# Attention and mixture of experts in one kernel: transposes, value products, sums and gates of a unit moved into two slots

## The chip, the cores and the metric

The kernel runs on one core of one Trainium2 chip. The metric is the device time of one execution in microseconds. The kernel before takes 1141.43 us, the median of three runs (1140.6 to 1145.1). One further execution was profiled; it took 1139.65 us, and the span of its instructions is 1137.9 us.

Engines are named as the profile names them: PE (TensorE, matrix products and transposes), PEld (its weight loads), DVE (VectorE), ACT (ScalarE), POOL (GpSimd) and SP (SyncE, which here only issues DMAs).

## The reference, cut to what matters

Attention over 8 batches and 12 heads of 448 rows of 64 numbers, with a normalisation of q and k, followed by a routed layer of 8 experts over the 3584 rows that come out. All is float32.

```
q_n, k_n = (rmsnorm(q, g_q), rmsnorm(k, g_k))
scores = scale * np.matmul(q_n, k_n.transpose(0, 1, 3, 2))
scores = scores - np.max(scores, axis=-1, keepdims=True)
attn = np.exp(scores)
attn = attn / (np.sum(attn, axis=-1, keepdims=True) + 1e-09)
attn_out = np.matmul(attn, v)
x = attn_out.transpose(0, 2, 1, 3).reshape(B * S, H * D)
logits = x @ w_gate + modality_bias[modality_id]
e_idx = np.argmax(logits, axis=1)        # one expert for each row
h = np.maximum(x[mask] @ w1[e], 0.0)
out[mask] = gate_w[mask, None] * (h @ w2[e])
```

## The kernel before, in words

**Units and slots.** Two heads of one batch are a unit, so there are 48 units. The main loop walks through slots: unit `u` has the seven slots `7u` to `7u+6`, and slot number `n` has the place `j = n mod 7` in its unit, called j0 to j6 below. In the slot (u, j) the kernel always does the scores of one seventh of unit u, transposed (`st`, two products on PE, four at j3), their exponential on ACT (`exp`, written to `p`), and for a later unit one seventh of the scores in the other orientation (`sa`, one product on PE) with the row maximum over them on DVE.

**What a unit needs besides.** The table `PLAN` gives, for each other kind of work, how many slots before or after the start of its unit it is due; it is spread over the slots by `put`:

- `tr`: four transposes of the normalised k (`tk`) or q (`tq`) into one PSUM tile, then an evacuation in four steps. `a0` (ACT) copies the whole tile, `dve` (DVE) subtracts that copy from the tile, `a1` and `a2` (ACT) copy one half each. The steps that read one PSUM tile are run one after another, so `dve` waits for `a0` and `a1` waits for `dve`. After `a0` and `dve` SP issues DMAs that put the halves where the products want them.
- `mt`: one transpose of the row maxima, copied out by ACT (`ms`) and moved by a DMA.
- `av`: the products of the exponentials with the values, in four parts c0 to c3, all into one PSUM tile, copied out by ACT after c3 (`avcopy`).
- `sums` (once in two units) and `gates` (once in four): products with 32 columns that gather the row sums and the routing logits in one PSUM tile, copied out by ACT after the gates.
- `recips` (once in four units): four transposes of that copy (`sp` in the profile), read by DVE.
- `xt`: four transposes of an `avcopy`, scaled out by DVE; every third one starts a store.

**What sets the order.** Nothing is scheduled by the compiler: each engine runs its instructions in the order in which the loop emits them. Within slot n the loop emits on PE first `st`, then `sa`, then the other work of the slot in the order in which the code names it. On ACT and DVE it runs `pre["A"]` and `pre["V"]` of the slot, then the exponential and the row maximum, then `post`. The function `at(where, n, fn)` puts a step there.

**Buffers.** PSUM has eight banks here: two for `st` (pool `ps_s`), two for `sa` (`ps_a`), two that `tr`, `mt`, `recips` and `xt` share (`ps_t`), one for sums and gates (`ps_m`) and one for `av` (`ps_o`). So the `st` of a slot waits until the exponential of two slots earlier is done, and a transpose that finds both `ps_t` banks taken waits until one has been read out.

**After the attention**, from 592.8 us on, the experts run: blocks of 256 rows, two matrix products in three parts each (`ph`, `py`), with weights split by ACT and DVE. The change doesn't touch that stage.

Of the kernel before, what the change touches and what calls it, by code (L numbers as in the profile page):

```python
# [30 lines left out]
NT1 = NB1 * S  # L31
BIG = float(1 << 20)
ET = mybir.EngineType
PLAN = {'rtj': 6, 'rushat': 36, 'av': (1, 1, 4, 6), 'xt': 4, 'xte': (2, 5), 'sm': 2, 'la': 6, 'rc': 9, 'csv': (1,), 'csj': (3, 6), 'csd': (1, 1), 'cse': (2, 1), 'sa': 14, 'mt': 6, 'tk': 21, 'tq': 18, 'nq': 26, 'nk': 26, 'sk': 49, 'sq': 50, 'rs': 48, 'ld': 58, 'first': {('sq', 0): -22, ('sk', 0): -22, ('nk', 0): -21, ('nq', 0): -20, ('sq', 1): -21, ('sk', 1): -21, ('sq', 2): -20, ('sk', 2): -20, ('nk', 1): -18, ('nq', 1): -18, ('tk', 0): -18, ('tq', 0): -18, ('sa', 0): -14, ('tk', 1): -13, ('tq', 1): -11, ('sa', 1): -7, ('mt', 0): -6, ('tk', 2): -8, ('tq', 2): -8, ('nq', 2): -14, ('nk', 2): -14, ('nq', 3): -2, ('nk', 3): -1, ('sq', 3): -8, ('sk', 3): -8, ('sq', 4): -9, ('sk', 4): -9, ('sq', 6): -6, ('sk', 6): -4, ('sk', 7): -7, ('sq', 8): 5, ('sk', 8): 5, ('nk', 7): 15, ('nq', 9): 31, ('tq', 3): 4, ('mt', 1): 0, ('nq', 5): 10, ('mt', 8): 50, ('rs', 0): -21, ('rs', 2): -18, ('nq', 8): 35, ('rs', 5): -7, ('mt', 2): 8, ('nq', 7): 18, ('mt', 5): 30, ('sk', 9): 15, ('tk', 9): 43, ('mt', 6): 36, ('nq', 6): 13, ('sa', 5): 22, ('rs', 7): 0, ('rs', 8): 6, ('mt', 4): 22, ('nk', 4): 4, ('ld', 9): 6, ('tk', 5): 15}, 'rs0': {0: 0, 2: 1, 5: 0, 7: 0, 8: 2}, 'sastep': 1, 'start': -22, 'warm': {5: 2, -6: 16, -12: 4, -7: 2, -9: 4, -21: 4}, 'warmn': 2, 'early': 1, 'late0': 1, 'pmp0': 2, 'ramp': 10, 'pmp': (0, 0, 1, 1, 1, 0, 1), 'nv': [(2, 1)], 'pmpa': (1, 0, 1, 0, 1, 1, 1), 'rush': (1, 1, 1), 'ps': [(7, 1)], 'pa': [(6, 0), (6, 1), (5, 1), (5, 0)], 'rtr': 6, 'sml': 4}
MANUAL = {ET.PE, ET.DVE, ET.Activation, ET.Pool, ET.SP}
IOFF = bass.IndirectOffsetOnAxis

# [29 lines left out]
def kernel(  # L67
# [15 lines left out]
    V, A, G = (Deferred(e, n) for e, n in ((nc.vector, "op"), (nc.scalar, "act"), (nc.gpsimd, "dma")))  # L83
# [562 lines left out]
    if True:  # L646
# [33 lines left out]
        def sumsq(u, i):  # L680
# [150 lines left out]
        def mt(u):  # L831
            t = T[u]
            ps = ps_t.tile([128, 512], F32, tag="t", name=f"mt{u}")
            PE.transpose(ps[0:NJ, :128], t["mx"], idn)
# [214 lines left out]
        P = PLAN  # L1049
# [6 lines left out]
        puts, done, routed = [], [], []  # L1056
# [71 lines left out]
        P = PLAN  # L1128
# [39 lines left out]
        for n in range(P["start"], NJ * NU):  # L1168
            i, j = divmod(n, NJ)
            todo = {}  # L1170
            for what, *a in plan.get(n, ()):
                todo.setdefault(what, []).append(tuple(a))
            state["n"] = n
            state["rush"] = i >= P["rushat"]
            warm(P["warm"].get(n, 0))
            ex = st(i, j) if 0 <= i < NU else None
            sm = [sa(*a) for a in todo.get("sa", ())]
            if n < 0:
                warm(P["warmn"])
            for u, c in todo.get("av", ()):  # L1180
                av(u, c)
                if c == 3:
                    at(pre["A"] if j else post, n + (j > 0), lambda u=u: avcopy(u))
            for a in todo.get("sums", ()):
                sums(*a)
            for a in todo.get("gates", ()):
                at(pre["A"], n + 1, gates(*a))
            for a in todo.get("tr", ()):
                a0, a1, a2, d_ = tr(*a)
                if a[0] < P["early"]:  # L1190
                    at(pre["A"], n + 1, a1)
                    at(pre["A"], n + 1, a2)
                    at(pre["A"], n + P["late0"], a0)
                    at(pre["V"], n + P["late0"], d_)
                    continue
# [196 lines left out]
    nv = nc.values_load(state["nsl"], min_val=0, max_val=NS1 + NS2)  # L1392
# [52 lines left out]
```

## Time and profile before

| | us |
|---|---|
| median of 3 runs (lowest to highest) | 1141.43 (1140.6 to 1145.1) |
| the profiled execution: its time | 1139.65 |
| span of its instructions | 1137.9 |
| PE busy in the span | 1089.8 (96%) |
| PEld busy | 856.9 (75%) |
| DVE busy | 863.7 (76%) |
| ACT busy | 827.7 (73%) |
| POOL busy | 656.8 (58%) |

A matrix product shows in the profile from its start to a modelled end, and products overlap. The distance from one start to the next is therefore what tells how long PE needs for it, and a busy share of 96% doesn't say that PE is at its best. In the timeline, products that follow each other are merged in one row: the start of the first, the time to the end of the last, and how many. An fp32 product with 64 or 32 columns is shown as two.

### The profile page before, as it was taken

What the parts mean: (1) busy time and instruction counts of PE and PEld (TensorE: products, weight loads), DVE (VectorE), ACT (ScalarE), POOL (GpSimd) and SP (SyncE); (2) the same over time, 40 slices, a digit from 0 to 9 for tenths busy, and PEclk for the clock granted to TensorE, in tenths of its full rate; (3) what the DMA queues carried; (4) which work ended last, traced back from release to release, by engine and by line L of the source; (5) the groups of instructions that cost most, each with busy time, mean ns of one, the idle gap of its engine ahead of it and who ended that gap; (6) DMA issues with size and microseconds to landing.
All of it is one profiled execution on the core that took longest, in us unless ns stands there. A gap on an engine that the chain in (4) does not pass through costs nothing. (4 is left out here: it accounts for less than half of the span.)

```text
span 1137.9 us, 19896 instructions
## 1 busy us (share of the span) xinstructions
PE 1089.8 (96%) x6678; PEld 856.9 (75%) x6678; DVE 863.7 (76%) x1598; ACT 827.7 (73%) x1605; POOL 656.8 (58%) x665
## 2 busy tenths in 40 slices
PE   7899999999999999999999999999999999999993
PEld 6655655566565565555568899999999999999981
DVE  4676778988779988789688987767777677776770
ACT  6878888778787787775666677668776687766770
POOL 4577677777777787777764565444244433345430
PEclk8899999999999999999999999999999999999996
DMA  7656567666576666665725111111161111111360
GB/s 170 169 127 154 127 174 173 167 161 148 141 180 162 163 144 160 168 147 114 212 66 189 26 46 59 40 57 56 43 252 41 56 43 56 32 40 56 115 186 11
DMA packets 101345, 131.78 MB, mean 116 GB/s; under 512 B 29979, under 2 KB 95983, under 8 KB 99696
## 3 DMA queue, kind: packets, MB, share of 16 engines
q1 hardware_dynamic: 83588, 88.57, 32.0%
q0 software_dynamic: 17616, 41.80, 11.7%
q8 instruction: 57, 0.93, 0.4%
q14 instruction: 56, 0.46, 0.1%
q10 hardware_dynamic: 28, 0.01, 0.0%
HBM read 148.74 MB, written 22.38 MB: 150 GB/s over the span
## 5 line engine op out<-in xcount | busy, mean ns | idle before, releaser
L485 PE MATMUL ph<-xw,w1w 128*128 128x256 f32 x2016 | 246.1, 283 | 1.8 <-DVE hlw L52 1.0
L485 PEld LDWEIGHTS ph<-xw,w1w 128*128 128x128 f32 x2016 | 243.9, 192 | 3.8 <-issue 1.4
L52 DVE TENSOR_REDUCE at_hlw<-sa 128x1 f32<-128x448 f32 x336 | 206.9, 618 | 48.3 <-PE sa L823 30.0
L52 DVE TENSOR_TENSOR w1w<-r,w1w 128x256 fp32r<-128x256 f32 x360 | 221.0, 672 | 13.8 <-ACT w1w L52 13.5
L52 ACT CAST w1w<-r 128x256 fp32r<-128x256 f32 x360 | 224.8, 722 | 0.0
L851 PE MATMUL st<-w1w 128*128 128x448 f32 (+1 forms) x480 | 191.7, 448 | 1.1 <-ACT r2w L52 0.8
L851 PEld LDWEIGHTS st<-w1w 128*128 128x128 f32 (+1 forms) x480 | 107.3, 239 | 45.1 <-ACT r2w L52 21.2
L52 ACT ACTIVATE hhw<-ph 128x512 fp32r<-128x512 f32 x56 | 33.5, 598 | 121.8 <-PE ph L485 121.8
L52 POOL TENSOR_TENSOR r2w<-r2w 128x448 f32<-128x448 f32 (+1 forms) x72 | 82.4, 1144 | 68.4 <-DVE r2w L52 30.6
L52 ACT ACTIVATE r2w<-st 128x448 f32<-128x448 f32 x168 | 90.0, 541 | 40.7 <-PE st L851 35.7
L823 PE MATMUL sa<-w1w 128*128 128x448 f32 (+1 forms) x288 | 110.6, 385 | 8.9 <-DVE at_hlw L52 5.8
L515 PE MATMUL py<-w2lw,hhw 128*128 128x384 f32 x448 | 113.9, 335 | 0.0
L851 PE MATMUL st<-w1w,w2ha 65*128 65x448 f32 x288 | 102.5, 376 | 3.1 <-DMA r2w<-in_v_dram 2.5
L52 ACT ACTIVATE at_w2lw<-st 128x448 f32<-128x448 f32 x168 | 89.3, 540 | 13.4 <-PE st L851 11.6
L52 POOL TENSOR_TENSOR xrw<-r,at_hlw 112x512 f32<-112x512 f32 x95 | 97.4, 1045 | 2.5 <-PE tr L752 2.2
L52 POOL DMA_INDIRECT out_dram<-yw,lb_oi x22 | 28.3, 1286 | 122.0 <-ACT yw L52 118.9
L515 PEld LDWEIGHTS py<-w2lw,hhw 128*128 128x128 f32 x448 | 80.9, 188 | 0.0
L52 DVE SCALAR_TENSOR_TENSOR hlw<-ph,hhw 128x512 fp32r<-128x512 f32 x56 | 38.7, 691 | 51.9 <-ACT hhw L52 51.9
L52 ACT ACTIVATE w1w<-tr,gs 64x448 fp32r<-64x448 f32 x96 | 60.3, 629 | 23.0 <-DVE xw L52 22.3
L52 POOL TENSOR_TENSOR r2w<-r2w,at_w2lw 64x448 f32<-64x448 f32 (+1 forms) x48 | 54.9, 1144 | 38.0 <-DVE r2w L52 19.5
L851 PEld LDWEIGHTS st<-w1w,w2ha 65*128 65x128 f32 x288 | 70.9, 246 | 5.4 <-DMA r2w<-in_v_dram 2.7
L52 ACT ACTIVATE xrw<-r 112x512 f32<-112x512 f32 (+1 forms) x124 | 64.6, 526 | 9.7 <-DMA r<-in_k_dram 7.2
(297 smaller groups left out, 2297.9 us busy)
## 6 DMA issues: line engine op xcount, KB each, us to landing
w1w<-xw SPq DMA_DIRECT2D x312, 112.0 KB
r<-in_q_dram SPq DMA_DIRECT2D x48, 224.0 KB
r<-in_k_dram SPq DMA_DIRECT2D x48, 224.0 KB
w2ha<-xw SPq DMA_DIRECT2D x72, 112.0 KB
x_d<-at_w2hb SPq DMA_DIRECT2D x8, 672.0 KB
x_d<-yw SPq DMA_DIRECT2D x8, 672.0 KB
r2w<-in_v_dram SPq DMA_DIRECT2D x16, 288.0 KB
at_w2lw<-in_v_dram SPq DMA_DIRECT2D x16, 288.0 KB
```

The lines of the kernel that those rows point to most:

```text
L52: return fn(*a, **kw)
L485: PE.matmul(ps[:, i], lhsT=lt_, rhs=rt_[:, c], start=n == 0, stop=n == 17)
L515: PE.matmul(ps[n][:, :384], lhsT=lt_[:, j, 128 * t : 128 * t + 128], rhs=rt_[:, 384 * n : 384 * n + 384], start=j == 0 and m == 0, stop=j ...
L823: PE.matmul(ps[:, :S], lhsT=t["qq"][r, h, a : a + 128], rhs=t["kk"][h][r], start=True, stop=True)
L851: PE.matmul(ps[:, :S], lhsT=l, rhs=t["qq"][:, h] if first else t["ql"][:, h], start=first and (j != 3 or h == 0), stop=not first and (j != ...
```

## The change

Six numbers of `PLAN` change, and a block of the loop's code moves. Taken modulo 7, the numbers place the work of a unit so:

| work | before | after |
|---|---|---|
| transposes of k (`tk`) | j0 | j1 |
| maxima transposed (`mt`) | j1 | j1 |
| `recips`, once in four units, nine of twelve times | j2 | j1 |
| products c0, c1 | j1 | j1 |
| transposes of q (`tq`) | j3 | j4 |
| `xt` | j4 | j4 |
| product c2 | j4 | j4 |
| product c3 | j6 | j4 |
| `sums`, once in two units | j2 | j4 |
| `gates`, once in four units | j6 | j4 |

For the last twelve units sums and gates stood at j4 already, and `recips` keeps j6 there. Within a slot the transposes are now emitted ahead of the products, sums and gates. The evacuation of `tr` starts in its own slot: `a0` and `dve` stand in `post` of the slot of the transposes, `a1` in `pre` of the next one and `a2` in `post` of that. Before, these were `pre` of the next slot, `post` of the next slot and `pre` of the one after.

```
-'av': (1, 1, 4, 6) ... 'sm': 2, 'la': 6, 'rc': 9 ... 'tk': 21, 'tq': 18 ... ('nq', 9): 31
+'av': (1, 1, 4, 4) ... 'sm': 4, 'la': 4, 'rc': 8 ... 'tk': 20, 'tq': 17 ... ('nq', 9): 32

             sm = [sa(*a) for a in todo.get("sa", ())]
             if n < 0:
                 warm(P["warmn"])
+            for a in todo.get("tr", ()):
+                a0, a1, a2, d_ = tr(*a)
...
+                at(post, n, a0)
+                at(post, n, d_)
+                at(pre["A"], n + 1, a1)
+                at(post, n + 1, a2)
+            for a in todo.get("mt", ()):
+                at(pre["A"], n + 1, mt(*a))
+            for a in todo.get("recips", ()):
...
+            for a in todo.get("xt", ()):
+                at(pre["V"], n + 1, xt(*a))
             for u, c in todo.get("av", ()):
                 av(u, c)
...
             for a in todo.get("gates", ()):
                 at(pre["A"], n + 1, gates(*a))
-            for a in todo.get("tr", ()):
-                a0, a1, a2, d_ = tr(*a)
...
-                at(pre["A"], n + 1, a0)
-                at(pre["V"], n + 1, d_)
-                at(post, n + 1, a1)
-                at(pre["A"], n + 2, a2)
-            for a in todo.get("mt", ()):
...
-            for a in todo.get("recips", ()):
...
-            for a in todo.get("xt", ()):
```

Three places show how the rows move. The first is PE in unit 14, slots j1 and j2, where `recips` is due (`sp2`). Names carry the unit's number, `tr17_1` being the k of unit 17; a wait stands in brackets, named after the engine that ends it. Before:

```order
L851 MATMUL st14_1_2201<-w1w_136 128x448 [waits Activation_49]
L851 MATMUL st14_1_2201<-w1w_136,w2ha_139 128x448
L823 MATMUL sa16_1_2204<-w1w_136 128x448 [waits DVE_49]
L890 MATMUL av13_2206<-at_w2lw_142,r2w_138 64x448 [waits Activation_49]
L890 MATMUL av13_2206<-at_w2lw_142,r2w_138 64x448 x3
L834 MATMUL mt15_2211<-idn_66,at_hlw_144 7x128
L851 MATMUL st14_2_2223<-w1w_136 128x448 [waits Activation_49]
L851 MATMUL st14_2_2223<-w1w_136,w2ha_139 128x448
L823 MATMUL sa16_2_2226<-w1w_136 128x448 [waits DVE_49]
L905 MATMUL sm3_2228<-at_hhw_143,sel_76 32x448 [waits PE_49]
L905 MATMUL sm3_2228<-at_hhw_143,sel_76 32x448
L905 MATMUL sm3_2228<-at_w2lw_142,sel_76 32x448 [waits Pool_49] x2
```

And after, slot j1 of the same unit up to the `st` of j2:

```order
L851 MATMUL st14_1_2196<-w1w_136 128x448 [waits Activation_49]
L851 MATMUL st14_1_2196<-w1w_136,w2ha_139 128x448
L823 MATMUL sa16_1_2199<-w1w_136 128x448 [waits DVE_49]
L752 MATMUL tr17_1_2201<-idn_66,xrw_135 128x112 [waits PE_49,Pool_49]
L752 MATMUL tr17_1_2201<-idn_66,xrw_135 128x112 x3
L834 MATMUL mt15_2206<-idn_66,at_hlw_144 7x128
L924 MATMUL sp2_2208<-idn_66,at_hlw_144 112x128 [waits Activation_49]
L924 MATMUL sp2_2208<-idn_66,at_hlw_144 112x128 x3
L890 MATMUL av13_2213<-at_w2lw_142,r2w_138 64x448 [waits PE_49]
L890 MATMUL av13_2213<-at_w2lw_142,r2w_138 64x448 x3
L851 MATMUL st14_2_2227<-w1w_136 128x448
L851 MATMUL st14_2_2227<-w1w_136,w2ha_139 128x448
```

The k transposes, `mt` and `recips` now stand in one slot and use the two `ps_t` banks three times: `sp2` gets the bank of `mt15`, and the wait in its row is for the ACT copy of `mt15`. Before, `recips` stood one slot later, behind the sums.

The second place is ACT around that copy, `xw_137<-mt15` (`ms`). The rows from `tr17_1` are `a0`, `a1` and `a2`, those from `st` the exponentials, those into `xrw` the squares for the norm. Before:

```order
L52 ACTIVATE r2w_138<-st14_0_2182 128x448
L52 ACTIVATE xrw_135<-r1_1_134 112x512
L52 ACTIVATE xw_137<-tr17_1_2187,gs_78 128x448
L52 ACTIVATE r2w_138<-st14_1_2201 128x448
L52 ACTIVATE w1w_136<-tr17_1_2187,gs_78 64x448 x2
L52 CAST xw_137<-mt15_2211 7x128
L52 ACTIVATE r2w_138<-st14_2_2223 128x448
```

After:

```order
L52 ACTIVATE r2w_138<-st14_0_2184 128x448
L52 ACTIVATE xrw_135<-r1_1_134 112x512
L52 ACTIVATE r2w_138<-st14_1_2196 128x448
L52 ACTIVATE xw_137<-tr17_1_2201,gs_78 128x448
L52 ACTIVATE w1w_136<-tr17_1_2201,gs_78 64x448
L52 CAST xw_137<-mt15_2206 7x128
L52 ACTIVATE r2w_138<-st14_2_2227 128x448
L52 ACTIVATE w1w_136<-tr17_1_2201,gs_78 64x448
```

Before, an exponential stood between `a0` and `a1`; now they follow each other directly, and one of the half copies comes after the next exponential.

The third place is ACT in the last slots of unit 14, j4 to j6, in the change: `tr17_0` is the q of unit 17, and each half copy has a small 64x64 one with it.

```order
L52 ACTIVATE r2w_138<-st14_4_2259 128x448
L52 CAST xw_137<-tr17_0_2264 128x448
L52 CAST w1w_136<-tr17_0_2264 64x448
L52 CAST w2ha_139<-tr17_0_2264 64x64
L52 COPY at_w2lw_142<-av13_2213 128x448
L52 ACTIVATE r2w_138<-st14_5_2294 128x448
L52 CAST w1w_136<-tr17_0_2264 64x448
L52 CAST w2ha_139<-tr17_0_2264 64x64
L52 ACTIVATE r2w_138<-st14_6_2312 128x448
```

Before, both pairs of half copies stood together ahead of the exponential of j5, and those of j5 and j6 followed each other; now one pair stands between them.

More of the change, by code (lines that the diff above doesn't have):

```diff
@@ L33 @@
 ET = mybir.EngineType
-PLAN = {'rtj': 6, 'rushat': 36, 'av': (1, 1, 4, 6), 'xt': 4, 'xte': (2, 5), 'sm': 2, 'la': 6, 'rc': 9, 'csv': (1,), 'csj': (3, 6), 'csd': (1, 1), 'cse': (2, 1), 'sa': 14, 'mt': 6, 'tk': 21, 'tq': 18, 'nq': 26, 'nk': 26, 'sk': 49, 'sq': 50, 'rs': 48, 'ld': 58, 'first': {('sq', 0): -22, ('sk', 0): -22, ('nk', 0): -21, ('nq', 0): -20, ('sq', 1): -21, ('sk', 1): -21, ('sq', 2): -20, ('sk', 2): -20, ('nk', 1): -18, ('nq', 1): -18, ('tk', 0): -18, ('tq', 0): -18, ('sa', 0): -14, ('tk', 1): -13, ('tq', 1): -11, ('sa', 1): -7, ('mt', 0): -6, ('tk', 2): -8, ('tq', 2): -8, ('nq', 2): -14, ('nk', 2): -14, ('nq', 3): -2, ('nk', 3): -1, ('sq', 3): -8, ('sk', 3): -8, ('sq', 4): -9, ('sk', 4): -9, ('sq', 6): -6, ('sk', 6): -4, ('sk', 7): -7, ('sq', 8): 5, ('sk', 8): 5, ('nk', 7): 15, ('nq', 9): 31, ('tq', 3): 4, ('mt', 1): 0, ('nq', 5): 10, ('mt', 8): 50, ('rs', 0): -21, ('rs', 2): -18, ('nq', 8): 35, ('rs', 5): -7, ('mt', 2): 8, ('nq', 7): 18, ('mt', 5): 30, ('sk', 9): 15, ('tk', 9): 43, ('mt', 6): 36, ('nq', 6): 13, ('sa', 5): 22, ('rs', 7): 0, ('rs', 8): 6, ('mt', 4): 22, ('nk', 4): 4, ('ld', 9): 6, ('tk', 5): 15}, 'rs0': {0: 0, 2: 1, 5: 0, 7: 0, 8: 2}, 'sastep': 1, 'start': -22, 'warm': {5: 2, -6: 16, -12: 4, -7: 2, -9: 4, -21: 4}, 'warmn': 2, 'early': 1, 'late0': 1, 'pmp0': 2, 'ramp': 10, 'pmp': (0, 0, 1, 1, 1, 0, 1), 'nv': [(2, 1)], 'pmpa': (1, 0, 1, 0, 1, 1, 1), 'rush': (1, 1, 1), 'ps': [(7, 1)], 'pa': [(6, 0), (6, 1), (5, 1), (5, 0)], 'rtr': 6, 'sml': 4}
@@ new lines @@
+PLAN = {'rtj': 6, 'rushat': 36, 'av': (1, 1, 4, 4), 'xt': 4, 'xte': (2, 5), 'sm': 4, 'la': 4, 'rc': 8, 'csv': (1,), 'csj': (3, 6), 'csd': (1, 1), 'cse': (2, 1), 'sa': 14, 'mt': 6, 'tk': 20, 'tq': 17, 'nq': 26, 'nk': 26, 'sk': 49, 'sq': 50, 'rs': 48, 'ld': 58, 'first': {('sq', 0): -22, ('sk', 0): -22, ('nk', 0): -21, ('nq', 0): -20, ('sq', 1): -21, ('sk', 1): -21, ('sq', 2): -20, ('sk', 2): -20, ('nk', 1): -18, ('nq', 1): -18, ('tk', 0): -18, ('tq', 0): -18, ('sa', 0): -14, ('tk', 1): -13, ('tq', 1): -11, ('sa', 1): -7, ('mt', 0): -6, ('tk', 2): -8, ('tq', 2): -8, ('nq', 2): -14, ('nk', 2): -14, ('nq', 3): -2, ('nk', 3): -1, ('sq', 3): -8, ('sk', 3): -8, ('sq', 4): -9, ('sk', 4): -9, ('sq', 6): -6, ('sk', 6): -4, ('sk', 7): -7, ('sq', 8): 5, ('sk', 8): 5, ('nk', 7): 15, ('nq', 9): 32, ('tq', 3): 4, ('mt', 1): 0, ('nq', 5): 10, ('mt', 8): 50, ('rs', 0): -21, ('rs', 2): -18, ('nq', 8): 35, ('rs', 5): -7, ('mt', 2): 8, ('nq', 7): 18, ('mt', 5): 30, ('sk', 9): 15, ('tk', 9): 43, ('mt', 6): 36, ('nq', 6): 13, ('sa', 5): 22, ('rs', 7): 0, ('rs', 8): 6, ('mt', 4): 22, ('nk', 4): 4, ('ld', 9): 6, ('tk', 5): 15}, 'rs0': {0: 0, 2: 1, 5: 0, 7: 0, 8: 2}, 'sastep': 1, 'start': -22, 'warm': {5: 2, -6: 16, -12: 4, -7: 2, -9: 4, -21: 4}, 'warmn': 2, 'early': 1, 'late0': 1, 'pmp0': 2, 'ramp': 10, 'pmp': (0, 0, 1, 1, 1, 0, 1), 'nv': [(2, 1)], 'pmpa': (1, 0, 1, 0, 1, 1, 1), 'rush': (1, 1, 1), 'ps': [(7, 1)], 'pa': [(6, 0), (6, 1), (5, 1), (5, 0)], 'rtr': 6, 'sml': 4}
@@ L1179 @@
                 warm(P["warmn"])
+            for a in todo.get("tr", ()):
+                a0, a1, a2, d_ = tr(*a)
+                if a[0] < P["early"]:
+                    at(pre["A"], n + 1, a1)
+                    at(pre["A"], n + 1, a2)
+                    at(pre["A"], n + P["late0"], a0)
+                    at(pre["V"], n + P["late0"], d_)
+                    continue
+                at(post, n, a0)
+                at(post, n, d_)
+                at(pre["A"], n + 1, a1)
+                at(post, n + 1, a2)
+            for a in todo.get("mt", ()):
+                at(pre["A"], n + 1, mt(*a))
+            for a in todo.get("recips", ()):
+                at(pre["V"], n + 1, recips(*a))
+                at(pre["V"], n + 1, lambda a=a: done.append(a[0]))
+            for a in todo.get("xt", ()):
+                at(pre["V"], n + 1, xt(*a))
             for u, c in todo.get("av", ()):
@@ L1187 @@
                 at(pre["A"], n + 1, gates(*a))
-            for a in todo.get("tr", ()):
-                a0, a1, a2, d_ = tr(*a)
[L1190 to L1195, printed above, removed]
-                at(pre["A"], n + 1, a0)
-                at(pre["V"], n + 1, d_)
-                at(post, n + 1, a1)
-                at(pre["A"], n + 2, a2)
-            for a in todo.get("mt", ()):
-                at(pre["A"], n + 1, mt(*a))
-            for a in todo.get("recips", ()):
-                at(pre["V"], n + 1, recips(*a))
-                at(pre["V"], n + 1, lambda a=a: done.append(a[0]))
-            for a in todo.get("xt", ()):
-                at(pre["V"], n + 1, xt(*a))
             if puts and n >= puts[0][0] and n - lastput[0] >= 3:
```

## The prediction

> **What bounds the kernel now.** I read the page first, then one quiet unit in PE's timeline, then ACT's timeline of the same stretch, and last the stretches in which PE's clock was lowered. The page:
>
> ```profile
> span 1137.9 us, 19896 instructions
> PE 1089.8 (96%) x6678; PEld 856.9 (75%) x6678; DVE 863.7 (76%) x1598; ACT 827.7 (73%) x1605; POOL 656.8 (58%) x665
> ...
> PEclk8899999999999999999999999999999999999996
> ```
>
> PE is nearly always occupied. The change touches the attention stage alone, and there the windows and groups give the length of a unit: 32 transposes of maxima, one in each unit, in 374.2 us, so 11.69 us each.
>
> ```profile
> 154.00:528.20 374.20, 367.92 (x1921) 219.16 (x1917) 314.22 (x624) 293.05 (x642) 281.09 (x301) 0.99 0.64 155
> ...
> L834 PE MATMUL mt<-idn,at_hlw 128*7 128x128 f32 x32 | 8.8, 275 | 0.0
> ```
>
> The columns behind the length are the busy times of PE, PEld, DVE, ACT and POOL. PE is idle for only 6.3 us. DVE is busy for 84% and ACT for 78%, so a unit could get shorter by some 15% before they stop it on average; but they are idle because they wait for PE, and the order in which they get their work counts. One quiet unit, from PE's timeline:
>
> ```profile
> 304.25 0.37 PE L823 MATMUL sa<-w1w 128*128 128x448 f32 x1
> 304.55 0.97 PE L890 MATMUL av<-at_w2lw 64*64 64x448 f32 x4
> 305.45 0.74 PE L851 MATMUL st<-w1w 128*128 128x448 f32 x2
> 306.03 0.37 PE L823 MATMUL sa<-w1w 128*128 128x448 f32 x1
> 306.24 0.55 PE L752 MATMUL tr<-idn,xrw 112*128 112x112 f32 x4
> 306.56 0.73 PE L851 MATMUL st<-w1w 128*128 128x448 f32 x2
> 307.12 0.37 PE L823 MATMUL sa<-w1w 128*128 128x448 f32 x1
> 307.42 1.72 PE L890 MATMUL av<-r2w,at_w2lw 128*64 128x448 f32 x8
> 309.08 0.28 PE L834 MATMUL mt<-idn,at_hlw 128*7 128x128 f32 x1
> 309.11 0.73 PE L851 MATMUL st<-w1w 128*128 128x448 f32 x2
> 309.68 0.37 PE L823 MATMUL sa<-w1w 128*128 128x448 f32 x1
> ...
> 310.70 0.37 PE L818 MATMUL sa<-xw,w2ha 128*128 128x448 f32 x1
> ...
> 311.80 0.37 PE L823 MATMUL sa<-w1w 128*128 128x448 f32 x1
> 312.10 0.97 PE L890 MATMUL av<-r2w,at_w2lw 128*64 128x448 f32 x4
> 313.00 0.65 PE L947 MATMUL xt<-idn,at_hlw 128*112 128x128 f32 x4
> 313.41 0.71 PE L851 MATMUL st<-w1w 128*128 128x448 f32 x2
> 313.96 0.37 PE L823 MATMUL sa<-w1w 128*128 128x448 f32 x1
> 314.17 0.57 PE L851 MATMUL st<-w1w 128*128 128x448 f32 x2
> 314.58 0.37 PE L823 MATMUL sa<-w1w 128*128 128x448 f32 x1
> ```
>
> No row names a wait: here PE sets the pace. A plain slot takes 0.62 us (`sa` to `sa`, 313.96 to 314.58).
>
> **What the change takes from PE.** Every change of kind costs PE something beyond the products. Value products run as pairs; eight last 1.72 us and four 0.97 us, so a pair costs 0.375 us. By the time from `sa` to `sa`, less a plain slot, less the work:
> - c3 alone (304.25 to 306.03): 1.78 - 0.62 - 0.75 = 0.41.
> - c0, c1 and `mt` (307.12 to 309.68): 2.56 - 0.62 - 1.50 - 0.11 = 0.33, with a transpose of 128 columns at (0.65 - 0.32) / 3 = 0.11.
> - c2 and `xt` (311.80 to 313.96): 2.16 - 0.62 - 0.75 - 0.44 = 0.35.
> - k transposes (306.03 to 307.12) and q transposes (310.70 to 311.80): 1.09 and 1.10, less 0.62 and four times about 0.095: 0.09 and 0.10. The 0.095 is (0.55 - 0.26) / 3, with 0.26 us for one transpose.
>
> That is 1.28 us in a unit. In the change two groups are left, each entered from transposes and left into `st`, for at most 0.41 each, and c3 follows c2 with other partitions; for that I take the 0.10 that the step from products to `mt` takes over the pace of pairs (309.08 - 307.42 = 1.66, against 1.50 and 0.05 of start-up). After: 0.92. The gain is 0.36, and with `sums`, which no longer stand alone every second unit, some 0.42 us. If entering from transposes is free (0.15 of each 0.41), it is 0.72; if c2 to c3 costs a whole 0.41, it is 0.1. Over 44 units (the first three fill the pipeline, the last ends outside the loop): **-18 us**, between -31 and -4.
>
> **What it puts on ACT's path.** ACT in the unit above:
>
> ```profile
> 307.25 0.63 ACT L52 ACTIVATE xw<-tr,gs 128x448 fp32r<-128x448 f32 x1
> 307.77 0.54 ACT L52 ACTIVATE at_w2lw<-st 128x448 f32<-128x448 f32 x1
> 309.18 1.27 ACT L52 ACTIVATE w1w<-tr,gs 64x448 fp32r<-64x448 f32 x2 [0.86 <-DVE xw L52]
> 310.48 0.25 ACT L52 CAST xw<-mt 7x128 fp32r<-7x128 f32 x1
> ...
> 313.55 0.53 ACT L52 CAST w1w<-tr 64x448 fp32r<-64x448 f32 x1
> 313.98 0.20 ACT L52 CAST xw<-tr 64x64 fp32r<-64x64 f32 x1
> 314.22 0.55 ACT L52 ACTIVATE at_w2lw<-st 128x448 f32<-128x448 f32 x1
> ...
> 314.92 0.53 ACT L52 ACTIVATE at_w2lw<-st 128x448 f32<-128x448 f32 x1
> 315.35 0.62 ACT L52 ACTIVATE xrw<-r 112x512 f32<-112x512 f32 x1
> ```
>
> The work of PE is now lumped. From the first `st` of j5 to the first `st` of the next j1 PE has three plain slots, 0.79 + 0.62 + 0.62 = 2.03 us (the first longer, since the second `st` behind a product group starts 0.37 after the first). That `st` of j1 needs the bank that the exponential of j6 frees. ACT can't begin the exponential of j5 before its second `st` ends, at about 0.37 + 0.37 + 0.10 = 0.84; exponential to next instruction is 0.43 (314.92 to 315.35), the pair of half copies, which the change puts there, 0.67 (313.55 to 314.22), the exponential of j6 0.54. Sum 2.48, with the release 2.53: PE waits 0.5 us in each unit. Before, the half copies stood ahead of both exponentials and long slots lay between. To this comes DVE: `a1` now follows `a0` directly, so ACT stands idle for the whole of DVE's subtraction and for what DVE still has ahead of it (0.86 us of wait in the row above, even with an exponential in between). ACT then reaches the exponential of j2 about when the `st` of j4 needs its bank; 0.05 to 0.3 us of wait there. I take 0.55 us in 43 units: **+24 us**, between 9 (0.2: the half copies overlap as exponentials do) and 39 (0.9: DVE late by a row maximum as well). The copy out of `av` and the gates' copy stay covered by PE's own j4; without that cover each would add its 0.5 us.
>
> **What it puts on PE itself.** In nine units `recips` finds both `ps_t` banks taken by the transposes of its own slot, and waits for ACT's copy of the maxima, `xw<-mt`. In ACT's queue that stands behind `a0`, DVE's subtraction and `a1`. DVE's row:
>
> ```profile
> 308.47 0.67 DVE L52 SCALAR_TENSOR_TENSOR xw<-tr,gs,xw 128x448 fp32r<-128x448 f32 x1
> ```
>
> So 0.63 + 0.67 + 0.63 + 0.25 = 2.18 us, with the hand-overs (0.04 each) and the tail of the transposes 2.4 us in which PE has nothing, since the products c0 and c1 and the `st` of j2 stand behind `recips` in its queue. If ACT comes late to the slot, as the paragraph above has it, it still has two squares and two exponentials ahead of `a0` (about 1.9 us, against 1.2 until the transposes are done): 3.2 us. I take 2.9: nine times, **+26 us**, between 22 and 30. Before, the same transposes came one slot later and behind the sums.
>
> A wait of this length touches the clock too. The longest wait of a quiet stage before:
>
> ```profile
> 292.71 0.64 PE L823 MATMUL sa<-w1w 128*128 128x448 f32 x1 [1.11 <-DMA w1w<-xw]
> ...
> 289.37:292.78 3.41, 2.27 (x13) 0.77 (x11) 1.27 (x3) 2.52 (x5) 0.98 (x2) 1.00 0.61 119
> ...
> 292.78:296.19 3.41, 3.41 (x12) 2.19 (x14) 2.01 (x4) 1.83 (x4) 2.43 (x3) 0.50 0.58 156
> ```
>
> PE was idle for 1.14 of 3.41 us, and for the next 3.41 us the granted clock was 0.50 (the third number from the end). A wait of 2.9 us leaves at least 1.45 us in one such stretch. A lowered stretch costs up to 1.7 us, less what falls into the wait itself: 1.0, nine times, **+9 us**, between 0 and 15. The Trainium skill (TensorE: Matmul & The Clock Gate, Part 1: The HAM clock gate) lets the clock fall after an idle window of about 3.4 us; by that, 2.9 us would not be enough, and the sum would be 9 us lower. The row above, with 1.14 us idle, disagrees with it.
>
> **DMAs.** The moves that SP issues behind `a0` and `dve` start one to two us later against the `sa` that needs them, and stand behind the same loads and stores. Units wait for such moves now (the 1.11 above); with units that are longer these waits shrink. I take -5 of the 6.3 us in which PE idled, between -6 and +6.
>
> **Sum.** -18 + 24 + 26 + 9 - 5 = +36 on 1139.65 us: **1176 us**. The median of the runs before is 1.8 us above the profiled time, which is within their spread. The experts' stage gets the same instructions.
>
> **The rivals.**
> - *The clock holds* through the nine waits, because a wait has to fill a stretch of 3.4 us to lower it: 1176 - 9 = 1167. For it: the quiet stage shows one such fall only, and a wait of 2.9 us fills no stretch. Against it: in that one case 1.14 us sufficed. 0.15. This is what the Trainium skill's page of the sentence above would have.
> - *ACT keeps up*: half copies and exponentials overlap and the `st` waits 0.2 us: -18 + 9 + 22 + 5 - 5 = +13, so 1153. For it: ACT is busy for only 78%. 0.12.
> - *All cancels*: entering products from transposes is free (-31), ACT's waits are small (+9), `recips` costs its least (+22), the clock holds and the DMA waits stay: 1140. 0.13. So ends also the case in which the new places of the evacuation change nothing but the order of names, ACT reaching each step when it did before.
> - *Faster*: the change of kind is what PE pays for, and the long slots j1 and j4 let ACT and DVE catch up, so that no `st` ever waits. Its place is the exits into `st` that disappear; its price -31, with `recips` at +22 and -5 of the DMA waits: -14, so 1126. It decides if the gain in a unit passes 0.5 us (9 x 2.4 over 44) while the run of three plain slots costs nothing. Against it: 2.53 us of ACT's work in 2.03 of PE's. 0.15.
>
> **How the numbers follow.** My forecast has 0.45. All cases but the last two are slower by over 0.5%, which is about what a measurement of this kernel can tell from no change: 0.72 slower, 0.13 the same, 0.15 faster. The forecast's own range is 1160 to 1200 (1139.65 with 20 to 60: low where DVE is never late and the clock recovers during the waits, high where both bounds of ACT's and PE's waits add up in part). The range reaches down to 1134, where the faster case begins, and leaves out that case and a little above 1200.
>
> **What would show it.** Right: nine waits of `sp` for `ACT xw` of 2.4 to 3.3 us in the waits, granted clock 0.50 behind most; a wait of about half a us ahead of the `st` of j1 in every unit; `sa` to `sa` around the j1 and j4 groups shorter in sum than now; normal units of about 11.3 us, those with `recips` near 15. Wrong: `sp` starting at once behind `mt`, three plain slots in 2.03 us, or DVE as the engine that ends the waits of `sa`.

## The result, and the profile after

The changed kernel takes 1221.79 us, the median of four runs (1216.57 to 1222.56). The kernel before, on the same chip, takes 1143.26 us (four runs, 1140.6 to 1146.49). The ratio is 1.068, with a 95% interval of 1.063 to 1.072. The change costs 78 us where 36 were forecast, and the time lies above the range of 1134 to 1200.

The page of the changed kernel, with the span, the busy times and the row of the granted clock:

```profile
span 1220.4 us, 19840 instructions
...
PE 1124.0 (92%) x6678; PEld 875.8 (72%) x6678; DVE 856.2 (70%) x1598; ACT 819.4 (67%) x1605; POOL 655.3 (54%) x665
...
PEclk8899999899998989999899999999999999999997
```

The work is the same (6678 matrix instructions in both), but PE is now idle for 96 us of the span, 48 before, and the row of the clock has dips that it didn't have. Below, a unit lasts from its first `st` to the first `st` of the next. Units 10 to 41 fill this stretch of the changed kernel (the columns are the length, the busy times of PE, PEld, DVE, ACT and POOL, the granted clock, the DMA share and GB/s):

```profile
166.90:602.50 435.60, 393.88 (x1916) 232.06 (x1916) 305.41 (x621) 287.76 (x643) 279.76 (x301) 0.95 0.55 133
```

That is 13.61 us for a unit, against 11.69 before. From the start of unit 3 to that of unit 47 the attention stage grew by 76.4 us (504.5 to 580.9). The profiled span grew by 82.5; the other 6 us, 1.2 ahead of unit 3 and 4.8 behind the start of unit 47, were not followed up.

The length of a unit depends on what it carries, so the next table splits it by slots. It gives medians over units 10 to 35, from the first `st` of a slot to that of the next, in us. Every second unit has sums, one in four of all has gates, and one in four has sums and `recips`. The column `unit` is the sum of the seven medians, and so is every length of a unit below that isn't called a mean.

```
               j0    j1    j2    j3    j4    j5    j6   unit   mean unit
before
 no sums      1.10  2.55  0.77  1.34  2.18  0.76  1.61  10.32    10.35
 sums         1.10  2.54  1.74  1.43  2.16  0.76  1.61  11.35    11.67
 gates        1.10  2.55  0.77  1.34  2.16  0.76  2.50  11.19    11.82
 sums,recips  1.10  2.55  2.16  1.42  2.16  0.76  1.70  11.85    12.37
after
 no sums      1.23  3.03  0.78  1.37  3.51  0.80  0.65  11.37    11.60
 sums         1.23  3.03  0.79  1.25  4.39  0.79  0.65  12.13    12.24
 gates        1.23  3.03  0.78  1.27  4.40  0.79  0.65  12.15    12.13
 sums,recips  1.23  8.16  1.18  1.03  4.22  0.79  0.65  17.26    17.53
```

Two things happened. The units with `recips` grew by about 5 us, all of it in j1. All the others grew by 0.8 to 1.05 us in their medians, and by 0.3 to 1.25 in the mean.

**The units with `recips`.** PE's timeline in unit 14:

```profile
222.13 0.55 PE L752 MATMUL tr<-idn,xrw 112*128 112x112 f32 x4
222.51 0.27 PE L834 MATMUL mt<-idn,at_hlw 128*7 128x128 f32 x1
225.99 1.10 PE L924 MATMUL sp<-idn,at_hlw 128*112 128x128 f32 x4 [3.20 <-ACT xw L52]
227.03 3.25 PE L890 MATMUL av<-at_w2lw,r2w 128*64 128x448 f32 x8
230.21 0.74 PE L851 MATMUL st<-w1w 128*128 128x448 f32 x1
```

`sp` waits 3.20 us for ACT's copy of the maxima, with everything of PE behind it. Then the eight value products last 3.25 us, where 1.73 is their time at full clock (240.69 below). ACT in the same stretch shows what the copy, `xw<-mt`, stands behind:

```profile
223.21 0.64 ACT L52 ACTIVATE xw<-tr,gs 128x448 fp32r<-128x448 f32 x1
225.17 0.63 ACT L52 ACTIVATE w1w<-tr,gs 64x448 fp32r<-64x448 f32 x1 [1.32 <-DVE xw L52]
225.70 0.24 ACT L52 CAST xw<-mt 7x128 fp32r<-7x128 f32 x1
```

ACT itself waits 1.32 us between `a0` and `a1`, for DVE's subtraction. DVE shows why:

```profile
222.81 0.61 DVE L52 TENSOR_REDUCE at_hlw<-sa 128x1 f32<-128x448 f32 x1
223.34 0.67 DVE L52 TENSOR_REDUCE at_hlw<-xrw 112x8 f32<-112x512 f32 x1
223.94 0.61 DVE L52 TENSOR_REDUCE at_hlw<-sa 128x1 f32<-128x448 f32 x1
224.47 0.67 DVE L52 SCALAR_TENSOR_TENSOR xw<-tr,gs,xw 128x448 fp32r<-128x448 f32 x1
```

`a0` is done at 223.85, but DVE is then in the middle of one reduction and has another ahead of the subtraction. So one PE wait hangs on a chain through ACT, DVE and ACT again. The clock behind it, in its own windows of 3.41 us (granted clock third from the end):

```profile
220.91:224.32 3.41, 1.60 (x9) 1.09 (x8) 3.01 (x7) 2.91 (x6) 2.53 (x3) 1.00 0.41 129
224.32:227.74 3.42, 1.75 (x6) 0.99 (x8) 1.36 (x4) 0.77 (x2) 2.84 (x3) 0.51 0.61 134
227.74:231.15 3.41, 3.41 (x11) 1.32 (x8) 0.69 (x5) 0.00 (x0) 0.00 (x0) 0.50 0.01 1
```

The wait lies across the border of two windows. PE was busy for about half of each, and each is followed by a window at half clock, so behind this one wait two are lowered. Of the nine waits, five are followed by two lowered windows and four by one.

**All other units.** PE's timeline of a unit without sums (unit 15), up to its slot j4:

```profile
238.67 0.37 PE L823 MATMUL sa<-w1w 128*128 128x448 f32 x1
239.32 0.75 PE L851 MATMUL st<-w1w 128*128 128x448 f32 x2 [0.28 <-ACT r2w L52]
239.90 0.37 PE L823 MATMUL sa<-w1w 128*128 128x448 f32 x1
240.11 0.55 PE L752 MATMUL tr<-idn,xrw 112*128 112x112 f32 x4
240.49 0.27 PE L834 MATMUL mt<-idn,at_hlw 128*7 128x128 f32 x1
240.69 1.73 PE L890 MATMUL av<-r2w 128*64 128x448 f32 x8
242.35 0.74 PE L851 MATMUL st<-w1w 128*128 128x448 f32 x2
242.93 0.36 PE L823 MATMUL sa<-w1w 128*128 128x448 f32 x1
...
243.97 0.36 PE L818 MATMUL sa<-xw,w2ha 128*128 128x448 f32 x1
244.40 0.74 PE L851 MATMUL st<-w1w 128*128 128x448 f32 x2
244.98 0.37 PE L823 MATMUL sa<-w1w 128*128 128x448 f32 x1
...
248.50 0.37 PE L823 MATMUL sa<-w1w 128*128 128x448 f32 x1
```

The row at 239.32 is the `st` of j1, late because ACT hasn't freed its bank. From the `sa` before it to its start pass 0.65 us, where 0.21 is the pace (before, 313.96 to 314.17). The page shows 0.28 of these 0.44 us as idle, since the tail of the `sa` covers the rest. But this `st` also takes longer: from its start to the next `sa` pass 0.58 us, and before only 0.41 (314.17 to 314.58). The weight loads tell why. PEld after, and then before, at the same `st`:

```profile
239.31 0.43 PEld L851 LDWEIGHTS st<-w1w 128*128 128x128 f32 x2 [0.66 <-ACT r2w L52]
```

```profile
313.96 0.46 PEld L851 LDWEIGHTS st<-w1w 128*128 128x128 f32 x2
```

Before, the load starts at 313.96, together with the previous `sa` product, and 0.21 us ahead of its own product (314.17). After, the load itself is what waits for ACT, and it starts with the product (239.31 and 239.32). So nothing covers it, the second `st` starts 0.37 us behind the first in place of 0.20, and a late `st` costs 0.17 us more than its wait. The `st` of j4 shows the same: 244.40 stands 0.43 behind its `sa`, so 0.22 late, and takes 0.58 to the next.

The waits that end in the weight loads of `st`, and ACT's wait for the subtraction, from 150 to 680 us; after, and then before:

```profile
ACT w1w L52 <- DVE xw L52: 85.9, 72, 4.2
...
PEld st L851 <- ACT at_w2lw L52: 28.9, 50, 2.8
...
PEld st L851 <- ACT r2w L52: 22.7, 44, 1.3
PEld st L851 <- ACT xw L52: 19.7, 28, 0.7
```

```profile
ACT w1w L52 <- DVE xw L52: 39.6, 70, 4.4
...
PEld st L851 <- ACT r2w L52: 13.8, 20, 0.7
...
PEld st L851 <- ACT at_w2lw L52: 7.2, 12, 0.7
```

Before, none of these loads waits longer than 0.7 us. In the trace before, no `st` of units 10 to 35 that directly follows an `sa` has a load that starts with its product; after, 65 have. In these 65 the second product stands 0.38 us behind the first (median), in the 61 whose load runs ahead 0.20. And ACT waits 46 us longer for DVE in as many waits.

### The profile page after: what moved, and what is told of

The parts are those of the page before. It is cut to its first block, busy times and chain, and to the rows that moved or that the text cites. A ratio compares the mean times of both kernels' runs of the same rounds, so it can differ in the third digit from the quotient of the medians.

```text
span 1220.4 us, 19840 instructions
## 1 busy us (share of the span) xinstructions
PE 1124.0 (92%) x6678; PEld 875.8 (72%) x6678; DVE 856.2 (70%) x1598; ACT 819.4 (67%) x1605; POOL 655.3 (54%) x665
## 5 line engine op out<-in xcount | busy, mean ns | idle before, releaser
L485 PE MATMUL ph<-xw,w1w 128*128 128x256 f32 x2016 | 248.9, 285 | 3.1 <-DVE hlw L52 2.3
L485 PEld LDWEIGHTS ph<-xw,w1w 128*128 128x128 f32 x2016 | 246.7, 194 | 5.2 <-DVE hlw L52 2.5
L851 PEld LDWEIGHTS st<-w1w 128*128 128x128 f32 (+1 forms) x480 | 109.8, 241 | 138.4 <-ACT at_w2lw L52 35.2
L52 POOL TENSOR_TENSOR r2w<-r2w 128x448 f32<-128x448 f32 (+1 forms) x72 | 82.5, 1146 | 118.7 <-ACT r2w L52 48.8
L851 PE MATMUL st<-w1w,w2ha 65*128 65x448 f32 x288 | 102.6, 376 | 2.7 <-DMA r2w<-in_v_dram 2.4
L52 POOL DMA_INDIRECT out_dram<-yw,lb_oi x22 | 25.4, 1153 | 123.0 <-ACT yw L52 120.0
L52 ACT CAST w1w<-tr 64x448 fp32r<-64x448 f32 x96 | 50.6, 527 | 48.5 <-DVE xw L52 44.6
L52 DVE TENSOR_REDUCE at_hlw<-xrw 112x8 f32<-112x512 f32 x91 | 61.4, 680 | 30.0 <-ACT xrw L52 29.9
```

Source lines behind the costliest of these rows:

```text
L52: return fn(*a, **kw)
L485: PE.matmul(ps[:, i], lhsT=lt_, rhs=rt_[:, c], start=n == 0, stop=n == 17)
L851: PE.matmul(ps[:, :S], lhsT=l, rhs=t["qq"][:, h] if first else t["ql"][:, h], start=first and (j != 3 or h == 0), stop=not first and (j != ...
```

## The experiments

Each ratio is to the kernel before on the same chip, with its 95% interval. Edits of the table are given by the numbers that differ.

### The reciprocals: one slot group later

On the changed kernel, `recips` goes to the slot of j3, where a `ps_t` bank is free:

```
-'rc': 8
+'rc': 10
```

> The changed kernel with recips two slots later (j3 in place of j1), nothing else. Theory A (nine waits of recips behind ACT's copy of the maxima, 3.2 us each, and the half clock that follows, cost about 5 us each): the j1 slots of 8 to 9 us fall to about 3.0, the waits of sp vanish, no 0.50 stretches in the attention between 100 and 540 us, and the time falls by 9 x 5 = 45 us to about 1177 us. Rival B (the lumps make ACT and DVE late whatever recips do; the long waits only let them catch up): the other slots get longer in exchange, and the time falls by less than 25 us, to 1197 us or more.

Measured: 1184.69 us, ratio 1.036 (1.030 to 1.043), so 37 us less than the changed kernel. The `sp` wait is gone, j1 of these units falls from 8.16 to 3.03, and the mean unit of this kind from 17.53 to 13.70. That is nearer to the 45 us of theory A than to rival B's 25. The wait and the clock behind it are therefore worth these 37 us and, on top, what this version has in their place. It has something there, since the `xt` of j4 in the same unit now wants the bank that `recips` holds until DVE has read it:

```profile
220.49 0.55 PE L752 MATMUL tr<-idn,xrw 112*128 112x112 f32 x4
222.31 0.62 PE L947 MATMUL xt<-idn,at_w2lw 128*112 128x128 f32 x4 [1.27 <-DVE pf L53]
```

The row names `pf`, a small step of DVE right behind the last read of that bank. The mean unit of this kind is still 1.3 us longer than before (12.37), some 12 us in nine units; the rest of the 41 us over the kernel before has other causes.

### The late halves of q, without and with the reciprocals

On the changed kernel, `a2` of q goes ahead of the exponential of j5, where both halves stood before. The forecast had put the half copy between the exponentials of j5 and j6 into its sum for the late `st` of j1.

```
-                at(post, n + 1, a2)
+                at(post if a[1] else pre["A"], n + 1, a2)
```

> The changed kernel with both half copies of the transposed q ahead of the exponential of j5 (a2 of q in pre in place of post), nothing else. Theory A (the st of j0 and j1 wait because a pair of half copies stands between the exponentials of j5 and j6, and each late st also delays the second st by 0.17 us): slot j0 falls from 1.23 to about 0.65 to 0.75 us, j1 by 0.17 us, about 0.7 us in a unit, 44 units: 31 us less, about 1191 us. Rival B (the lumped order itself makes ACT late): the wait moves to another st, and the time stays within 8 us of 1222 us.

Measured: 1210.45 us, ratio 1.060 (1.054 to 1.066): 11 us less. Slot j0 falls from 1.23 to 0.79, which is the whole wait of the `st` of j1, and a unit without sums from 11.37 to 11.24 only (its mean grows, from 11.60 to 11.96). This is neither the 31 us less of theory A nor the 8 or less of its rival. ACT's lateness has moved a slot earlier, to the `st` of j0 and of j4 (j3 grows to 1.51 in these units).

> Both edits together: recips at j3, and both half copies of q ahead of the exponential of j5. Theory A: the two gains add up, 1222 - 45 - 31 = 1146 us (1138 to 1155), about as the kernel before. Rival B: 1185 us or more.

Both edits together: 1177.63 us, ratio 1.030 (1.024 to 1.035). On top of the later reciprocals, the halves are worth 7 us, and the two intervals overlap. The gains don't add up: theory A's 1146 is missed by 32 us, and the rival's 1185 by 7.

### The halves of k after the exponential

On top of both edits, `a1` of k goes behind the exponential of its slot, so that ACT doesn't stand and wait for DVE's subtraction ahead of an exponential that PE needs:

```
-                at(pre["A"], n + 1, a1)
+                at(post if a[1] else pre["A"], n + 1, a1)
```

> e3 (recips at j3, both half copies of q early, 1178 us) and, beside that, the first half copy of k behind the exponential of j2 (a1 of k in post). Theory A (st of j4 waits because that exponential stands behind DVE's subtraction and a1): the wait ahead of the st of j4 goes, 0.22 us and the exposed weight load of 0.17 us in a unit: 12 to 17 us less, about 1163 us. Rival D (by now DMA and DVE set the pace): within 6 us of 1178.

Measured: 1166.83 us, ratio 1.019 (1.014 to 1.023): another 11 us. Slots j1 and j3 are now as short as PE's work (2.86 and 1.02), and the plain unit lasts 10.89. So the wait between `a0` and `a1` did hold up the exponentials behind it, and the time comes near the 1163 of theory A. What remains are the units with `recips` (13.71 in the mean), where the `xt` wait is still there:

```profile
213.42 0.55 PE L752 MATMUL tr<-idn,xrw 112*128 112x112 f32 x4
216.14 0.62 PE L947 MATMUL xt<-idn,at_w2lw 128*112 128x128 f32 x4 [2.17 <-DVE pf L53]
```

### Reciprocals in j6

On top of the three edits, the reciprocals go to a slot of j6. The number counts from an earlier unit, so 6 is four slots earlier than 10, not further on as the expectation has it: what stood in j3 of unit 14 now stands in j6 of unit 13, which has the gates.

```
-'rc': 10
+'rc': 6
```

> The kernel with the k halves also moved (all three late steps undone: reciprocals apart, q halves early, k halves late), with the reciprocals of a fourth unit one slot group further on, in the slot of j6 in place of that of j3. Theory A: in the units with reciprocals the transposes (xt) that follow them wait up to 2.2 us for VectorE to read the bank of the maxima (216.14, 2.17 us in that kernel), a half clock follows, and these units last 13.7 us in the mean against 11.3; with the wait out of the way nine units lose 1.7 to 2 us each, some 15 us, and the time goes from 1167 to about 1150. Rival B: the wait only goes to the next user of the bank or of VectorE's time (the subtractions ahead of j0's exponentials are late instead), the units with reciprocals stay above 13 us and the time at 1162 or more.

Measured: 1161.91 us, ratio 1.019 (1.014 to 1.024). In the trace the `xt` wait of unit 14 is gone and the units that had it fall to 12.47 in the mean, where the kernel before has 12.37; those that have the reciprocals now, with the gates, stay as they were (11.89, and 11.80 without). The stage from unit 3 to unit 47 is 10.6 us shorter (520.3 against 530.9), but the execution profiled here is the fastest of its four and that of the edit before the second slowest. The medians differ by 5 us, and the ratios, each against the kernel before on its own chip, don't differ at all. So the units did as theory A has it and the time as rival B has it: the mechanism shows in the profile, but a gain in time isn't established. Some of the wait went where the rival expected it, to the next user of the bank and of DVE:

```profile
208.85 0.27 PE L834 MATMUL mt<-idn,at_hlw 128*7 128x128 f32 x1 [0.50 <-DVE lg L52]
...
213.78 0.48 PE L823 MATMUL sa<-w1w 128*128 128x448 f32 x1 [0.70 <-DVE at_hlw L52]
```

This version has units of 10.90 (no sums), 11.32 (sums), 11.47 (gates, now with `recips`) and 11.81 (sums, where `recips` stood), against 10.32, 11.35, 11.19 and 11.85 before. The `st` of j0 is still late in 21 of the 26 units 10 to 35, which lengthens j6 and j0.

### The old evacuation in the new places

On the changed kernel with the reciprocals in j3, the four steps of the evacuation go back to where they were, one slot later:

```
-                at(post, n, a0)
-                at(post, n, d_)
-                at(pre["A"], n + 1, a1)
-                at(post, n + 1, a2)
+                at(pre["A"], n + 1, a0)
+                at(pre["V"], n + 1, d_)
+                at(post, n + 1, a1)
+                at(pre["A"], n + 2, a2)
```

> The changed kernel with recips at j3 (as in e1) and, beside that, the evacuation of the transposes in its places of before (a0 and dve in pre of the next slot, a1 in post of it, a2 in pre of the one after); compared with e1 at 1185 us. Theory A (late exponentials in the run j5, j6, j0 delay st): now both pairs of half copies of q and DVE's subtraction stand around the exponentials of j5 and j6, so slot j0 gets 0.6 us longer still, and the time rises by about 25 us to 1205 to 1215 us. Rival C (a1 directly behind a0, idle for the whole of DVE's subtraction, is what makes ACT late; the lumps are harmless): the time falls to 1165 us or less.

Measured: 1183.46 us, ratio 1.036 (1.032 to 1.041), the same as with the new evacuation (1184.69). Slot j0 grows from 1.23 to 1.74, but j3 and j4 shrink (1.25 to 1.04, and 4.40 to 4.26), so that a unit with sums lasts 12.29 against 12.14. With the work in lumps, both orders make some `st` late, and here it hardly changes the sum which one. Neither the 1205 to 1215 us of theory A nor the 1165 of its rival came.

### The parts alone

From here on the edits are made to the kernel before. First the new evacuation alone, with everything else in its old slot:

> The kernel before with the evacuation of the change alone (a0 and dve in the slot of the transposes, a1 in pre of the next, a2 in post of it), all PE work at its old place and in its old order. Theory A: no run of plain slots lies behind a pair of half copies (long slots j1 and j4 follow), so PE is not delayed: 1137 to 1152 us, though ACT's wait for DVE's subtraction rises from 40 us to 70 or more. Rival C (ACT's idle time behind a0 costs by itself, about 0.5 us in a unit): 1165 us or more.

Measured: 1153.78 us, ratio 1.010 (1.006 to 1.014). Units of the common kinds keep their medians (11.35 and 11.20 for sums and gates); those with `recips` grow from 11.85 to 12.22, and those without sums from 10.32 to 10.59. ACT's wait for DVE's subtraction rises to 57.6 us (39.6 before), and the time lies just above the 1152 of theory A.

Then only the value product c3, sums and gates in j4 (`'av': (1, 1, 4, 4)`, `'sm': 4`, `'la': 4`):

> The kernel before with one part of the change alone: product c3, sums and gates at j4 (the places that the change gives them), while transposes, recips, their order in the slot and the evacuation stay as before. By the PE rows, an isolated c3 group costs 0.41 us beyond its work and joined to c2 0.1, sums alone 0.2 in every second unit: 0.3 to 0.4 us less in a unit, 13 to 18 us, if no engine is late: about 1127 us. Rival B (lumps make ACT or DVE late): 1143 us or more, since the slots j5 to j3 then hold less of PE's work and the st wait there.

Measured: 1152.23 us, ratio 1.007 (1.004 to 1.010). The medians of the four kinds of unit add up to 44.90 us, against 44.71 before: what gathering saves on PE is given back inside the units, as the rival expected.

Then only c3 in j4 (`'av': (1, 1, 4, 4)`):

> The kernel before with product c3 alone moved from j6 to j4; sums and gates stay at j2 and j6. Theory A (an isolated group costs 0.41 us, joined to c2 0.1; gates still need a group of their own in one unit of four; no long run of plain slots but j5, j6): 0.2 to 0.3 us less in a unit, 1131 to 1137 us. Rival E (as in e4, waits for DMAs and exponentials take back what PE saves): 1141 us or more.

Measured: 1146.39 us, ratio 1.003 (1.001 to 1.006). Slot j6 gives back 0.96 us and j4 takes 0.92, so gathering c3 saves 0.04 us in a unit, and the time shows nothing of it, as the rival expected. Slot j0 keeps its 1.10 though no products stand ahead of its `st` any more: in 21 of 26 units that `st` itself now comes with a late load.

Last, the changed kernel with its products, sums and gates back in their old slots, so that the transposes and the evacuation alone are moved (`'av': (1, 1, 4, 6)`, `'sm': 2`, `'la': 6`, and `'rc': 10`):

> The change without its gathering of products: transposes at j1 and j4, first in their slot and evacuated in it, recips at j3, but c3 at j6, sums at j2 and gates at j6 as before. If the parts add up, e1 less e4's loss: 1185 - 8 = about 1177 us. Theory A: c3 at j6 makes the run j5, j6, j0 long again for PE (1.2 us more), so st of j0 and j1 are no longer late: 1155 us or less. Rival (the transposes' place and not the run is what costs): 1175 us or more.

Measured: 1163.6 us, ratio 1.018 (1.011 to 1.024). Slot j6, which has c3 again, lasts 1.61 in place of 0.65, and j0 is down to 0.79: with one long slot between j5 and j1, ACT is in time for the `st` of j1. The time lies between theory A (1155) and its rival (1175). The units with `recips`, again in j3 and with the `xt` wait, last 14.15 in the mean against 12.37, some 16 of the 22 us over the kernel before.

### ACT relieved

Is it the amount of ACT's work that makes `st` late, or its order? In two kernels the exponential works on 64 of 448 columns from unit 2 on, where it takes 0.22 us in place of 0.54: the changed kernel with the reciprocals in j3, and the kernel before. The rest of the exponential is left out, so the routing behind it differs and only the attention stage is compared.

```
-                A.activation(out=t["p"][:, j], in_=ps[:, :S], func=AF.Exp)
+                w = S if u < 2 else 64
+                A.activation(out=t["p"][:, j, :w], in_=ps[:, :w], func=AF.Exp)
```

> e1 (the changed kernel with recips at j3) with the exponential of units 2 and later taken over 64 of its 448 columns; the rest of p keeps old values, so what follows is not the attention, and the routing differs. To be read by the attention stage alone, up to the st of the last unit (625.7 us after the start in e1). The exponential then takes about 0.2 us in place of 0.54, 2.3 us of ACT's work less in a unit. Theory A (ACT's lateness in the runs of plain slots makes st late): the normal unit without sums falls from 11.36 to about 10.2 us, j0 to 0.65, and the last unit starts at about 580 us. Rival D (the lumps themselves, DVE or the DMAs cost the time): it stays at 610 us or more.

> The kernel before with the same shortened exponential; the same holds for what it leaves out. Theory A: in its order ACT is hardly late, so PE's times stay: the unit without sums 10.2 to 10.32 us, the last unit starts at 572 to 582 us (582.2 before). With e9 it tells what the gathered order is worth to PE when ACT has time: by the PE rows 0.3 us in a unit, 10 us or more by which e9 comes before e10. Rival F (the gain of PE was never there): e9 and e10 start their last unit within 5 us of each other, or e9 later.

Measured, in one run each: 1168.97 us for the gathered order and 1148.63 for the old one. Units 10 to 41 in the windows: first the gathered order with the full exponential (the first experiment), then the gathered and the old order with the short one:

```profile
164.20:568.40 404.20, 379.48 (x1918) 227.14 (x1917) 303.86 (x622) 287.52 (x643) 279.26 (x301) 0.99 0.60 143
```

```profile
156.50:554.10 397.60, 370.64 (x1918) 227.91 (x1917) 306.56 (x624) 224.00 (x643) 279.00 (x301) 0.98 0.61 145
```

```profile
155.10:529.50 374.40, 367.04 (x1919) 219.41 (x1916) 310.45 (x624) 228.61 (x642) 281.34 (x301) 0.99 0.65 154
```

ACT's busy time (the fourth of the five) falls by a fifth, from 287.5 us and, in the kernel before, from 293.05. The old order gains nothing from it. In the gathered order j0 falls from 1.23 to 0.62, as it should if ACT's run of work is too long there, and the stage from 404.2 to 397.6; it is still 23 us behind the old one. The last unit starts at 608.6 us in the gathered order (625.7 with the full exponential), near the rival's 610 and far from the 580 of theory A, and 26 us later than in the old one, not 10 earlier.

What the short exponential doesn't shorten stands behind DVE: ACT's wait for the subtraction is 102.6 us (76.7 in the first experiment, both from 150 to 560 us), and the units with `recips` last 14.89 in the mean, against 13.70. So ACT's load makes up 6.6 us of the 30 by which this order lies behind in these units. The rest points to the chain through DVE, but no run relieved DVE, so that isn't shown.

This run also shows the late load by itself, at the `st` of j1 in unit 21:

```profile
291.03 0.25 PEld L851 LDWEIGHTS st<-w1w 128*128 128x128 f32 x1 [0.17 <-ACT r2w L52]
```

Its product starts in pace, at 291.04, 0.21 us behind the `sa`, and still the second product follows 0.36 us later, not 0.20.

## Why the prediction was wrong

**The direction and the two mechanisms that cost time (the wait of `recips`, and ACT's lateness) were right; the step that failed is the size of "What it puts on ACT's path", +24 us.** The term stood at 0.55 us in a unit, at most 0.9, and comes out at 1.2. From the tables: slot j0 has 0.61 over a plain slot of 0.62 (0.44 of wait for the `st` of j1, 0.17 of the load of a late `st` in j0); j1 has 3.03 against 2.86 once the halves were moved, j3 1.25 against 1.04, j4 4.39 against 4.22, and j6 0.03. That is 0.61 + 0.17 + 0.21 + 0.17 + 0.03 = 1.19. The waits alone, 0.44 + 0.21 + 0.03 = 0.68, are near the forecast of 0.50 for j1 and 0.05 to 0.3 for j4. What the working lacks is the 0.17 us that each of three late `st` adds because its weight load no longer hides behind the product ahead of it. In the kernel before, the 0.37 between two `st` appears behind value products, and I took it for a property of leaving the products; the 65 late loads behind `sa` show it without any products ahead. Over 43 units the term is 1.19 x 43 = 51 us. In the nine units with `recips` the `st` of j4 is in time (j3 1.03, j4 4.22), which takes off 3: 48 us, twice the forecast and above its bound of 39. The Trainium skill (TensorE: Matmul & The Clock Gate, Part 2: What happens when you issue a matmul) has the next tile's weights load while this tile's product runs. The trace agrees where the `st` is in time (load 0.21 us ahead of its product); where the load waits for ACT (0.66 us at 239.31), it starts with its product.

**The gain on PE, -18 us, was about right.** In unit 15 the five slots that carry moved work take 3.03 + 3.52 + 3 x 0.62 = 8.41 us from `sa` to `sa`, against 2.56 + 2.16 + 1.78 + 1.09 + 1.10 = 8.69 before. The gain is 0.28, where 0.36 stood; the second group costs more than assumed (3.52 - 0.62 - 1.50 - 0.44 - 0.38 = 0.58, not 0.51). Sums that share a slot save a further 0.05 on average. So 0.33 x 44 = 14 us.

**The `recips` wait, +26 us, was right.** Nine waits, 3.0 us each, with the engine that the forecast named, over the whole span:

```profile
PE sp L924 <- ACT xw L52: 27.2, 9, 3.6
```

**The clock, +9 us, was right in kind and too small.** A slot j1 with `recips` is 8.37 - 3.03 = 5.34 us longer in the mean. With 3.0 of wait and about 0.53 for four transposes at full clock (half of the 1.04 from 225.99 to 227.03, at half clock), some 1.8 us are left for the clock: 16 us, just outside the 0 to 15. I had counted one lowered window for each wait, and five of the nine waits lower two. The rival "the clock holds" is refuted nine times. Wait and clock make 43 us; the first edit, with less of both, gave 37 back.

**The DMA waits, -5 us**, are not borne out as such. PE's waits that end with a DMA come to 2.7 us in the attention stage before (2.1 for `sa`, 0.6 for `st`) and to 2.0 after; 3.1 us of the idle time before ended with DVE. What did get smaller is the excess of a unit's mean over its medians: 0.32, 0.63 and 0.03 us before and 0.11, -0.02 and 0.23 after in the three kinds without `recips`. That is 0.66 us in four units, 7 us in 44; what it consists of was not taken apart.

**The sum by these sizes:** -14 + 48 + 27 + 16 - 7 = +70, where the stage from unit 3 to unit 47 shows 76; 6 us stay open.

**The rivals.** "Faster" and "all cancels" both needed ACT to be in time. The relieved kernel shows that PE's gain of 0.3 us in a unit doesn't appear even when ACT has a fifth less to do. Of the signs named in the forecast, the normal unit of 11.3 us came out at 11.4 to 12.15 and the unit with `recips` at 17.3, not 15.

**What stays open.** With the three late steps moved and the reciprocals in j6, 1161.91 us is still 2% above the kernel before. The tables put this into the late `st` of j0 and into units with DMA or DVE waits, but no run took these away, so that is argued and not shown. No version tried was faster than the kernel before.

## What to carry to other kernels

Gathering work into few slots saves PE only its changes of kind (here 0.3 us in 11), and takes away the long slots in which the other engines catch up; before moving anything, add up what the slower engines must do during the longest run of short slots. A late product cost its wait and then its weight load, which had been hidden, so price a wait at each product with both. Before two uses of one bank are put into the same slot, follow the chain that frees it: a copy that stands behind a step which waits for another engine costs that engine's queue as well, and a wait of this length lowered the clock behind it, nine times of nine.

## What the runs showed of the hardware

- A weight load of 128x128 that waits for a semaphore is exposed: the second of two products follows 0.37 us behind the first, not 0.20, and the pair takes 0.58 us to the next product in place of 0.41.
- One wait of 3.2 us across the border of two clock windows was followed by two windows at half clock. PE was busy for 1.60 of 3.41 us and 1.75 of 3.42 us in them, and the granted clock was 0.51 and 0.50 in the two that followed. The Trainium skill (TensorE: Matmul & The Clock Gate, Part 1: The HAM clock gate) asks for an idle window of about 3.4 us; here neither window was idle for more than 1.81 us. But idle time in one window doesn't decide it alone: in the last stage of the same run a window with 1.82 us idle (1187.0 to 1190.4) is followed by one at 1.00.
- An exponential of 64 columns takes 0.22 us and one of 448 takes 0.54 (means of 224 in units 10 to 41), and ACT's busy time falls by 63.5 us over these 224, so 0.28 each.
